# Attention stage of an attention and two-layer expert kernel: mantissa part of the weight conversion in a PSUM bank of its own

## Chip, cores and metric

One core of one Trainium2 chip. The metric is device microseconds of one launch. The kernel before took 845.74 us (median of 3 runs, 844.73 to 848.07).

## What is computed

Three stages in float32, on weights that arrive as float64:

```python
q_d, k_d, v_d = (x.reshape(B, H, Sd, 4, D).mean(axis=3) for x in (q, k, v))
out_up = np.repeat(sm_attn(q_d, k_d, v_d), 4, axis=2)
scores = np.where(abs(i - j) < 4, scale * (q @ k.T), -1e9)
x = out_up + softmax(scores) @ v
x = np.maximum(np.maximum(x @ w1, x @ w2), x @ w3) @ w_out
out = ((x @ w_a) * (x @ w_b)) @ w_out2
```

q, k and v are 4 x 8 x 576 x 64; the two later stages see 2304 tokens of width 512, with inner widths of 768 and 1536.

## The kernel before

**Stages.** Attention runs over 16 items (a batch and a pair of heads). For each item `a_load_qk` and `a_load_v` (L212 to L267) issue the loads on SP's queue, `a_qk` (L284) brings q and k into transposed form (items 0 to 7 by PE through PSUM, items 8 to 15 by DVE's transposes L291 and L292), `a_scores` (L330) makes the pooled and the windowed scores with their softmax, `a_tr` (L410) sums v over groups of four on POOL (L414, L415) and transposes the weights, and `a_av` (L445) multiplies by v and adds. Its POOL work is L396 (`ed`) and L403 (`el`, softmax by its sum), L414 and L415 (`vr`, `vd`), and L497 (`xl`, the low part of the result). One tile each of `k`, `q`, `vr` and `vw` serves items 8 to 15, so a load waits for the last reader of the item before.

**Dense work in attention.** From the fifth item on, products of the first layer (`dense`, tiles `ps_m`, L695) are put between the attention's matmuls. They need converted weights. Behind attention (from about 200 us) the order of work is written out by hand.

**Weight conversion.** `convert_steps` (L522) turns 512 columns of float64 into float32: L539 takes the exponent bits (`ce`) of the loaded tile `raw`, L542 the upper mantissa (`cm`), L546 (ACT) shifts the exponent, L547 adds the lower mantissa, L549 puts in the sign, L556 multiplies both. L561 and L562 then split the result into two parts. Eight pieces are converted in attention, one or two for each item named in `CONV_AT`. `raw` has two buffers, `ce` and `cm` one each.

**PSUM in attention.** `bk` hands out 8 banks: three under tag "t" (transposes of the weights, products with v) and five under tag "m" (transposes of q and k, scores, dense products). In the last stage `convert_steps` already keeps its mantissa in a bank, `ps_c`.

**Who sets the order.** In attention a scheduler orders the instructions of every engine by its own estimate of times and by which buffer is free; a change of buffers or of the order in `convert_steps` therefore moves other instructions too.

Of the kernel before, what the change touches and what calls it, by code (L numbers as in the profile page):

```python
# [15 lines left out]
ALU = mybir.AluOpType  # L16
# [48 lines left out]
def attn_moe_kernel(  # L65
# [14 lines left out]
    nc = tc.nc  # L80
# [47 lines left out]
    psp_ = {0: ps_ctx.enter_context(tc.tile_pool(name="psm", bufs=1, space=PSUM))}  # L128

    def bk(st, name):  # L130
        if 1 in psp_:
            return psp_[1].tile([P, 512], F32, tag="m", name=name, bufs=4)
        t, n = ("t", 3) if st in "tv" else ("m", 5)
        return psp_[0].tile([P, 512], F32, tag=t, name=name, bufs=n)


# [22 lines left out]
    for half in range(2):  # L159
        m = cap[half * 64 : half * 64 + 64]  # L160
        for sgn in (1, -1):
            nc.gpsimd.affine_select(
                out=m,
# [23 lines left out]
    st = [dict() for _ in items]  # L187
# [96 lines left out]
    def a_qk(i):  # L284
# [5 lines left out]
        if i >= TV:  # L290
# [6 lines left out]
            pool_qk(i, qp, n)  # L297
            return
        tail = bk("q", "ps_t2")
        pss = []  # L300
        for nm in ("k", "q"):
            ps = bk("q", "ps_t")
            for r in range(RF):
                nc.tensor.transpose(ps[:, r * P : (r + 1) * P], s[nm][:, r], ident)
            pss.append(ps)
# [24 lines left out]
    def a_scores(i):  # L330
        s = st[i]
        psd = bk("s", "ps_sd")
        pd = psd[: 2 * DQ, : NDQ * SD].rearrange("m (t k) -> m t k", t=NDQ)
        for t in range(NDQ):
# [187 lines left out]
    def convert_steps(key, w=None):  # L522

        r = raw.pop(key)
        lo, hi = r[:, :, 0], r[:, :, 1]
        top = r.rearrange("p n w -> p (n w)").bitcast(U16).rearrange("p (n w) -> p n w", w=4)[:, :, 3]
        late_n[0] += "p" in late
        pl = late["p"] if late_n[0] % 2 else rawp
        e = pl.tile([P, NP_], U16, tag="ce", name="ce", bufs=CB)
        fin = w  # L530
        if w is None or "c" not in psp_:
            m = pl.tile([P, NP_], F32, tag="cm", name="cm", bufs=CB)
            if w is None:
                fin = m
        if "c" in psp_:
            m = psp_["c"].tile([P, NP_], F32, tag="cs", name="ps_c", bufs=1)
        m = m.bitcast(U32)
        s16, f = e.bitcast(I16), m.bitcast(F32)
        nc.vector.tensor_scalar(  # L539
            out=e, in0=top, scalar1=0x7FF0, scalar2=None, op0=ALU.bitwise_and  # L540
        )
        nc.vector.tensor_scalar(  # L542
            out=m, in0=hi, scalar1=0x000FFFFF, scalar2=0x00100000, op0=ALU.bitwise_and, op1=ALU.bitwise_or
        )
        yield
        nc.scalar.activation(out=s16, in_=e, func=AF.Relu, bias=ebias, scale=8.0)  # L546
        nc.vector.scalar_tensor_tensor(out=f, in0=lo, scalar=2.0**-32, in1=m, op0=ALU.mult, op1=ALU.add)  # L547
        yield
        nc.vector.scalar_tensor_tensor(  # L549
            out=e, in0=top, scalar=0x8000, in1=e, op0=ALU.bitwise_and, op1=ALU.bitwise_or  # L550
        )
        yield
        i0, i1 = f, e.bitcast(BF16)
        if w is not None and len(w.shape) == 3:
            i0, i1 = (x.rearrange("p (a b) -> p a b", a=w.shape[1]) for x in (i0, i1))
        nc.vector.scalar_tensor_tensor(out=fin, in0=i0, scalar=2.0**-20, in1=i1, op0=ALU.mult, op1=ALU.mult)  # L556
        yield fin
# [6 lines left out]
    def convert_piece(key, h, l, q=None):  # L564
        for f in convert_steps(key):
            pass
        if ("q", q) in mark:
            with tc.issue_after(mark["q", q].ins):
                split(h, l, f)
        else:  # L570
            split(h, l, f)
# [70 lines left out]
    def conv1():  # L642

        key, _, h, l = inflight.pop(0)
        for f in convert_steps(key):
            if f is None:
                yield
        w_prefetch()
        yield
        nc.scalar.copy(h, f)  # L650
        yield
        nc.gpsimd.tensor_tensor(out=l, in0=f, in1=h.bitcast(F32), op=ALU.subtract)
        ready.add(key)
        yield
# [369 lines left out]
    def conv2_in(c, j):  # L1024


        def tt(eng, o, a, b, op):
            eng.tensor_tensor(out=F[:, o], in0=F[:, a], in1=F[:, b], op=op)  # L1028

        F = late["p"].tile([P, 8, KH], F32, tag="F", name="F", bufs=1)  # L1030
        for n, dst in enumerate((F[:, 0:2], F[:, 5:8:2])):
            take((2, c, j, n))
            for f in convert_steps((2, c, j, n), dst):
                yield
            ahead()
        tt(nc.vector, 3, 7, 5, ALU.add)
        tt(nc.gpsimd, 4, 0, 7, ALU.subtract)
        yield
        tt(nc.vector, 2, 3, 0, ALU.subtract)
        yield  # L1040
        tt(nc.gpsimd, 6, 1, 2, ALU.subtract)
        yield
        yield
        yield
        for g in range(2):
            if (c, j) < (1, 1):
                yield ("w", c + c + j)
            elif j == 1:
                yield ("a", 2 * c - 1, g)
            yield from split2(c, j, g, F[:, 3 * g : 3 * g + 3].rearrange("p a b -> p (a b)"))  # L1050
        yield from split2(c, j, 2, F[:, 6])
# [344 lines left out]
    for i in range(NI):  # L1396
# [4 lines left out]
        for x in LOOPS.get(i, LOOP).split():  # L1401
            f, d = x[0], int(x[1:])
# [267 lines left out]
```

## Time and profile before

| | |
|---|---|
| median of 3 runs | 845.74 us |
| profiled execution, its own time | 847.74 us |
| its span | 845.9 us |
| PE, busy share of the span | 97% |
| DVE | 78% |
| POOL | 52% |
| ACT | 42% |
| mean granted TensorE clock | 0.98 |

The span runs from the first to the last instruction of the profiled execution; 1.84 us of its time lie around it. PE is TensorE's matmuls, PEld its weight loads, DVE is VectorE, ACT is ScalarE, POOL is GpSimd, SP is the engine that issues most loads. Busy shares are means over stages with different limits, so a change to one stage is read from that stage.

### The profile page before, as it was taken

The page shows a single profiled execution, that of the slowest core. Times are in us where ns is not written, and L with a number is a line of the kernel's source. Part 1 is how long each engine was busy: PE and PEld are TensorE (multiplying, and loading weights), DVE is VectorE, ACT ScalarE, POOL GpSimd, SP SyncE. Part 2 cuts the span into 40 slices and gives each one's busy share as a digit, 9 for nine tenths or more (in the row PEclk, how much of TensorE's full clock was granted, in tenths as well). Part 3 has the DMA queues.
Part 4 walks back from the last instruction along what each step waited for, and adds up shares of the span by engine and source line. Part 5 has one row for each costly group of instructions (what it writes and reads, how often), then busy time and mean ns, then how long its engine had stood idle before and what let it go on. Part 6 is the DMA issues. An engine that isn't in the chain of part 4 may idle for free.

```text
span 845.9 us, 15426 instructions
## 1 busy us (share of the span) xinstructions
PE 818.5 (97%) x5785; PEld 767.7 (91%) x5785; DVE 656.6 (78%) x1220; ACT 355.2 (42%) x812; POOL 444.0 (52%) x417
## 2 busy tenths in 40 slices
PE   4888989999999999999999999999999999999998
PEld 3666778999999999999999999999999999999997
DVE  4899986854989688689689689798888845577775
ACT  3685654544343223324246544444433432333331
POOL 3875775445456335546557645545554543355541
PEclk8798989999999999999999999999999999999999
DMA  8997855410321111320144554454553458766612
GB/s 175 187 191 140 153 112 102 80 26 18 124 75 50 51 50 50 138 75 26 64 156 174 193 186 166 184 183 171 182 168 106 150 200 330 266 224 224 225 50 76
DMA packets 125557, 116.35 MB, mean 138 GB/s; under 512 B 81834, under 2 KB 108202, under 8 KB 125482
## 3 DMA queue, kind: packets, MB, share of 16 engines
q1 hardware_dynamic: 121162, 98.06, 39.4%
q10 hardware_dynamic: 4320, 17.30, 5.8%
q8 instruction: 45, 0.74, 0.4%
q14 instruction: 30, 0.25, 0.1%
HBM read 80.74 MB, written 34.60 MB: 136 GB/s over the span
## 4 chain that ended last, share of the span: by engine, by line
PE 85%; DMA 5%; POOL 4%; DVE 2%; SPq 2%; issue 1%; ACT 1%; POOLq 0%; DVEq 0%; ACTq 0%
PE ps_m L695 39%; PE ps_u L1086 30%; PE ps_q L860 5%; PE ps_m L1236 4%; DMA vr<-in_v_dram 4%; PE ps_av L473 1%; PE ps_ud L451 1%; POOL vr L414 1%; PE ps_tl L436 1%; POOL el L403 1%; PE ps_sd L335 1%; PE ps_s L353 1%; PE ps_m L860 1%; DMA raw<-in_moe_w_dram 1%; PE ps_td L425 1%
## 5 line engine op out<-in xcount | busy, mean ns | idle before, releaser
L695 PE MATMUL ps_m<-xh,w 128*128 128x384 f32 x864 | 175.0, 341 | 0.3 <-ACT xh L496 0.3
L695 PEld LDWEIGHTS ps_m<-xh,w 128*128 128x128 f32 x864 | 152.8, 190 | 2.1 <-ACT xh L496 0.6
L1086 PE MATMUL ps_u<-xh,w 128*128 128x384 f32 x720 | 136.8, 336 | 0.1
L1086 PEld LDWEIGHTS ps_u<-xh,w 128*128 128x128 f32 x720 | 125.3, 188 | 1.9 <-DVE acc L751 0.4
L1086 PE MATMUL ps_u<-xl,w 128*128 128x384 f32 x648 | 122.4, 335 | 0.4 <-ACT sn L1098 0.4
L1086 PEld LDWEIGHTS ps_u<-xl,w 128*128 128x128 f32 x648 | 112.9, 188 | 2.2 <-ACT sn L1098 0.7
L1098 ACT COPY sn<-ps_u 128x384 f32<-128x384 f32 x108 | 51.1, 479 | 123.7 <-PE ps_u L1086 120.2
L1276 POOL TENSOR_TENSOR gl<-g,gh 128x384 fp32r<-128x384 f32 x52 | 55.4, 1066 | 82.3 <-ACT gh L1275 75.2
L695 PE MATMUL ps_m<-xl,w 128*128 128x384 f32 x432 | 95.2, 339 | 1.7 <-POOL xl L497 1.7
L695 PE MATMUL ps_m<-wo,gh 128*128 128x512 f32 (+1 forms) x316 | 92.4, 390 | 0.0
L695 PEld LDWEIGHTS ps_m<-xl,w 128*128 128x128 f32 x432 | 76.9, 189 | 2.1 <-POOL xl L497 2.0
L695 PEld LDWEIGHTS ps_m<-wo,gh 128*128 128x128 f32 x316 | 58.4, 188 | 9.6
L724 DVE TENSOR_TENSOR t<-ps_m,t 128x384 f32<-128x384 f32 x48 | 26.5, 551 | 45.6 <-PE ps_m L695 40.3
L546 ACT ACTIVATE ce<-ce,ebias 128x512 int16<-128x512 uint16 x60 | 43.4, 724 | 43.0 <-DVE ce L539 42.9
L1017 POOL TENSOR_TENSOR w<-F,w 128x768 fp32r<-128x768 f32 (+1 forms) x36 | 56.1, 1573 | 9.2 <-ACT w L1015 8.7
L1345 DVE TENSOR_TENSOR acc<-ps_m,acc 128x512 f32<-128x512 f32 (+1 forms) x67 | 44.9, 676 | 18.1 <-PE ps_m L695 17.9
L549 DVE SCALAR_TENSOR_TENSOR ce<-raw,ce 128x512 uint16<-128x512 uint16 x60 | 49.8, 830 | 4.0 <-ACT ce L546 3.9
L1110 DVE TENSOR_TENSOR ca<-ps_u,sn 128x384 f32<-128x384 f32 x54 | 30.0, 555 | 29.4 <-PE ps_u L1086 18.1
L1028 POOL TENSOR_TENSOR F<-F 128x256 f32<-128x256 f32 x24 | 20.1, 839 | 59.3 <-DVE F L556 49.5
L695 PE MATMUL ps_m<-wo,gl 128*128 128x512 f32 (+1 forms) x158 | 48.9, 391 | 0.0
L1228 DVE TENSOR_TENSOR acc<-ps_m,acc 128x512 f32<-128x512 f32 (+1 forms) x62 | 33.3, 552 | 15.5 <-PE ps_m L1236 13.2
L539 DVE TENSOR_SCALAR ce<-raw 128x512 uint16<-128x512 uint16 x60 | 40.6, 677 | 2.2 <-DMA raw<-in_moe_w_dram 2.2
(209 smaller groups left out, 1687.4 us busy)
## 6 DMA issues: line engine op xcount, KB each, us to landing
dw<-w SPq DMA_DIRECT2D x24, 768.0 KB
raw<-in_moe_w_dram SPq DMA_DIRECT2D x18, 512.0 KB
raw<-in_moe_w_out_dram SPq DMA_DIRECT2D x18, 512.0 KB
w<-dw SPq DMA_DIRECT2D x12, 768.0 KB
w<-dw ACTq DMA_DIRECT2D x12, 768.0 KB
dw<-wo SPq DMA_DIRECT2D x12, 512.0 KB
vw<-in_v_dram SPq DMA_DIRECT2D x62, 80.0 KB
vr<-in_v_dram SPq DMA_DIRECT2D x16, 288.0 KB
```

The costliest lines, as they stand in the source:

```text
L539: nc.vector.tensor_scalar(out=e, in0=top, scalar1=0x7FF0, scalar2=None, op0=ALU.bitwise_and)
L546: nc.scalar.activation(out=s16, in_=e, func=AF.Relu, bias=ebias, scale=8.0)
L549: nc.vector.scalar_tensor_tensor(out=e, in0=top, scalar=0x8000, in1=e, op0=ALU.bitwise_and, op1=ALU.bitwise_or)
L695: nc.tensor.matmul(ps, lhs[a], rhs[b], start=(i == 0), stop=(i == n - 1))
L860: nc.tensor.matmul(ps, sw[c0, n][a][:, m * P : (m + 1) * P], hq[n][b], start=start and k == 0, stop=k == 2, skip_group_check=not start,)
L1017: nc.gpsimd.tensor_tensor(out=l, in0=w, in1=h.bitcast(F32), op=ALU.subtract)
L1086: nc.tensor.matmul(ps, w[:, a, slot, kk], y[:, b * HK + kk], start=start and i == 0, stop=i == 3 * HK - 1, skip_group_check=not start,)
L1098: nc.scalar.copy(t, ps)
L1228: nc.vector.tensor_tensor(out=a, in0=x, in1=a, op=ALU.add)
L1236: nc.tensor.matmul(y, lhs[a], tw[c, n][b], start=start and k == 0 and t == ts.start, stop=k == 2, skip_group_check=True,)
L1276: nc.gpsimd.tensor_tensor(out=l, in0=g, in1=h.bitcast(F32), op=ALU.subtract)
L1345: nc.vector.tensor_tensor(out=a, in0=ps, in1=a, op=ALU.add)
```

## The change

In attention the mantissa lies in a PSUM bank (tag "c", one buffer), the ring "m" has four banks in place of five, and the two mantissa instructions are written behind the exponent's and the sign's. Only the last multiply then writes the SBUF tile `cm`. Other stages convert as before.

```diff
-        t, n = ("t", 3) if st in "tv" else ("m", 5)
+        t, n = ("c", 1) if st == "c" else ("t", 3) if st in "tv" else ("m", 4)
...
+        attn = 1 not in psp_
+
+        def mantissa():
+            nc.vector.tensor_scalar(
+                out=m, in0=hi, scalar1=0x000FFFFF, scalar2=0x00100000, op0=ALU.bitwise_and, op1=ALU.bitwise_or
+            )
+
+        def low():
+            nc.vector.scalar_tensor_tensor(out=f, in0=lo, scalar=2.0**-32, in1=m, op0=ALU.mult, op1=ALU.add)
+
         if "c" in psp_:
             m = psp_["c"].tile([P, NP_], F32, tag="cs", name="ps_c", bufs=1)
+        elif attn:
+            m = bk("c", "ps_c")
...
-        nc.vector.tensor_scalar(
-            out=m, in0=hi, scalar1=0x000FFFFF, scalar2=0x00100000, op0=ALU.bitwise_and, op1=ALU.bitwise_or
-        )
+        if not attn:
+            mantissa()
         yield
         nc.scalar.activation(out=s16, in_=e, func=AF.Relu, bias=ebias, scale=8.0)
-        nc.vector.scalar_tensor_tensor(out=f, in0=lo, scalar=2.0**-32, in1=m, op0=ALU.mult, op1=ALU.add)
+        if not attn:
+            low()
         yield
         nc.vector.scalar_tensor_tensor(
             out=e, in0=top, scalar=0x8000, in1=e, op0=ALU.bitwise_and, op1=ALU.bitwise_or
         )
         yield
+        if attn:
+            mantissa()
+            low()
```

What the scheduler makes of it stands at three places.

DVE, from the additions behind item 3 to the transposes of item 8 (`ce`, `cm`, `ps_c` and `raw` are the conversion's tiles, `kt` and `k` the transpose's); in the kernel before:

```order
L483 TENSOR_TENSOR x_902<-ps_av,up 128x286
L539 TENSOR_SCALAR ce<-raw 128x512
L542 TENSOR_SCALAR cm<-raw 128x512
L273 TENSOR_REDUCE kd<-kt 128x144
L369 TENSOR_REDUCE md<-ps_sd 96x3
L547 SCALAR_TENSOR_TENSOR cm<-raw,cm 128x512
L549 SCALAR_TENSOR_TENSOR ce<-raw,ce 128x512
L386 TENSOR_REDUCE ml<-ps_s 128x5 x2
L291 STREAM_TRANSPOSE kt<-k 128x576
```

and now, from the same addition on:

```order
L551 TENSOR_SCALAR ce<-raw 128x512
L538 TENSOR_SCALAR ps_c<-raw 128x512
L400 TENSOR_REDUCE eps_118<-el 128x5
L315 TENSOR_REDUCE qp<-ps_t 128x128
L543 SCALAR_TENSOR_TENSOR ps_c<-raw,ps_c 128x512
L401 TENSOR_REDUCE sl<-eps_118 128x5
L561 SCALAR_TENSOR_TENSOR ce<-raw,ce 128x512
L315 TENSOR_REDUCE qp<-ps_t_1181 128x16
L273 TENSOR_REDUCE kd<-kt 128x144
L369 TENSOR_REDUCE md<-ps_sd 96x3
L402 RECIPROCAL sl<-sl 128x5
L571 SCALAR_TENSOR_TENSOR cm<-ps_c,ce 128x512
```

The fifth piece is converted as a whole before item 8's transpose, and a sixth (not shown) also stands ahead of it, where before one piece was still open.

SP, the loads around item 6's k and q (`raw` is a piece of weights); before:

```order
L518 DMA raw<-in_moe_w_dram 128x4x256
L231 DMA k<-in_k_dram 128x4x64
L243 DMA vr<-in_v_dram 72x4x256
L231 DMA k<-in_k_dram 128x4x64
L234 DMA k<-in_k_dram 64x2x64
L267 DMA vw<-in_v_dram 64x5x64 x4
L231 DMA q<-in_q_dram 128x4x64 x2
```

and now:

```order
L518 DMA raw<-in_moe_w_dram 128x4x256
L243 DMA vr<-in_v_dram 72x4x256
L267 DMA vw<-in_v_dram 64x5x64 x4
L518 DMA raw<-in_moe_w_dram 128x4x256
L231 DMA k<-in_k_dram 128x4x64 x2
L234 DMA k<-in_k_dram 64x2x64
L267 DMA vw<-in_v_dram 64x5x64 x4
L231 DMA q<-in_q_dram 128x4x64 x2
```

The sixth piece of weights (the second `raw` row) is now asked for right behind the fifth and one item's v, ahead of items 6 and 7's k and q; before it stood behind both of these. It waits for the fourth piece to be converted, since `raw` has two buffers.

PE, the scores of item 8 (`ps_s` and `ps_sd` are scores, `ps_m` dense products, all from the ring "m"); before:

```order
L335 MATMUL ps_sd<-kd,qd_92 96x144 x3
L695 MATMUL ps_m<-xh,w_141 128x384 x4
L695 MATMUL ps_m<-xl,w_140 128x384 x4
L340 LDWEIGHTS identb
L340 MATMUL ps_s<-cap,identb 128x320
L353 MATMUL ps_s<-kt,qt 58x61 x2
L353 MATMUL ps_s<-kt,qt 58x64 x3
L425 MATMUL ps_td<-ident,ed 72x96 x3
L340 LDWEIGHTS identb
L340 MATMUL ps_s<-cap,identb 128x320
L353 MATMUL ps_s<-kt,qt 58x64 x6
```

and now:

```order
L335 MATMUL ps_sd<-kd,qd_92 96x144 x3
L340 LDWEIGHTS identb
L340 MATMUL ps_s<-cap,identb 128x320
L353 MATMUL ps_s<-kt,qt 58x61 x2
L353 MATMUL ps_s<-kt,qt 58x64 x8
L340 LDWEIGHTS identb
L340 MATMUL ps_s<-cap,identb 128x320
L353 MATMUL ps_s<-kt,qt 58x64 x8
L353 MATMUL ps_s<-kt,qt 54x57 x2
```

The dense products that stood between the pooled and the windowed scores are gone from there, and one bank of scores is filled to its end before the other is begun, where before the second was opened while the first was still being written.

## Rows read from the trace of the kernel before

**Rows 1.** Stretches of the span: us, then busy us of PE, PEld, DVE, ACT, POOL; granted clock; DMA share, GB/s.

```profile
20.00:60.00 40.00, 34.24 (x463) 26.23 (x463) 37.38 (x99) 29.52 (x95) 31.02 (x31) 0.80 0.95 194
60.00:118.00 58.00, 50.60 (x640) 40.92 (x641) 55.44 (x120) 35.52 (x108) 40.78 (x45) 0.91 0.73 140
118.00:200.00 82.00, 82.00 (x960) 74.42 (x961) 51.59 (x135) 40.86 (x115) 41.02 (x50) 0.98 0.35 70
200.00:430.00 230.00, 229.01 (x1337) 227.24 (x1327) 185.93 (x308) 77.77 (x152) 118.08 (x97) 1.00 0.22 72
```

**Rows 2.** Costliest DVE groups, 0 to 120 us: busy us, mean ns of one, idle before.

```profile
L547 DVE SCALAR_TENSOR_TENSOR cm<-raw,cm 128x512 f32<-128x512 uint32 x8 | 9.8, 1231 | 0.0
L556 DVE SCALAR_TENSOR_TENSOR cm<-cm,ce 128x512 f32<-128x512 f32 x8 | 9.4, 1180 | 0.0
L539 DVE TENSOR_SCALAR ce<-raw 128x512 uint16<-128x512 uint16 x8 | 7.7, 964 | 2.2 <-DMA raw<-in_moe_w_dram 2.2
L549 DVE SCALAR_TENSOR_TENSOR ce<-raw,ce 128x512 uint16<-128x512 uint16 x8 | 6.5, 818 | 0.0
L542 DVE TENSOR_SCALAR cm<-raw 128x512 uint32<-128x512 uint32 x8 | 4.7, 586 | 0.0
```

**Rows 3.** The same groups, 430 to 700 us, where the mantissa lies in PSUM.

```profile
L547 DVE SCALAR_TENSOR_TENSOR ps_c<-raw,ps_c 128x512 f32<-128x512 uint32 x30 | 20.8, 692 | 0.7
L542 DVE TENSOR_SCALAR ps_c<-raw 128x512 uint32<-128x512 uint32 x30 | 20.5, 684 | 0.0
L556 DVE SCALAR_TENSOR_TENSOR cm<-ps_c,ce 128x512 f32<-128x512 f32 x10 | 6.8, 684 | 0.1
```

**Rows 4.** One long L547 in the timeline of DVE, then POOL beside it: start, us, what.

```profile
67.06 3.51 DVE L547 SCALAR_TENSOR_TENSOR cm<-raw,cm 128x512 f32<-128x512 uint32 x1
...
67.06 0.73 POOL L415 TENSOR_TENSOR vd<-vr 72x256 f32<-72x256 f32 x1
67.75 0.90 POOL L396 TENSOR_TENSOR ed<-ed,sd 96x432 f32<-96x432 f32 x1
68.61 1.40 POOL L403 TENSOR_TENSOR el<-el,sl 128x320 f32<-128x320 f32 x2
69.97 2.44 POOL L497 TENSOR_TENSOR xl<-x,xh 128x384 fp32r<-128x384 f32 x2
```

**Rows 5.** DVE's groups, 60 to 118 us.

```profile
L547 DVE SCALAR_TENSOR_TENSOR cm<-raw,cm 128x512 f32<-128x512 uint32 x4 | 6.8, 1694 | 0.0
L556 DVE SCALAR_TENSOR_TENSOR cm<-cm,ce 128x512 f32<-128x512 f32 x4 | 5.1, 1270 | 0.0
```

**Rows 6.** Chain of waits that ended last, 60 to 121 us: start, us, what.

```profile
68.00 2.48 issue
70.49 1.48 DVE ce L549
...
81.67 3.42 DMA vr<-in_v_dram
...
93.70 4.56 DMA vr<-in_v_dram
...
106.08 4.46 DMA vr<-in_v_dram
110.67 1.26 POOL vr L414
111.94 1.87 POOL el L403 x2
113.85 0.99 PE ps_tl L436 x5
```

**Rows 7.** Who waited for whom, 60 to 118 us: us in total, times, longest.

```profile
POOL vr L414 <- DMA vr<-in_v_dram: 14.6, 4, 6.0
PE ps_tl L436 <- POOL el L403: 3.5, 2, 3.1
PE ps_s L340 <- DVE el L387: 1.4, 2, 1.0
```

**Rows 8.** POOL's groups, 60 to 118 us, then 120 to 200 us.

```profile
L403 POOL TENSOR_TENSOR el<-el,sl 128x320 f32<-128x320 f32 x12 | 9.4, 797 | 0.0
L497 POOL TENSOR_TENSOR xl<-x,xh 128x384 fp32r<-128x384 f32 x6 | 7.1, 1182 | 0.0
...
L403 POOL TENSOR_TENSOR el<-el,sl 128x320 f32<-128x320 f32 x12 | 8.4, 719 | 0.6 <-DVE sl L402 0.6
L497 POOL TENSOR_TENSOR xl<-x,xh 128x384 fp32r<-128x384 f32 x7 | 7.3, 1050 | 0.3 <-ACT xh L496 0.2
```

## Prediction

> **What bounds the kernel now.** First the span in stretches [rows 1]. From 118 us on PE is busy without a gap (82.00 of 82 us, then 229.01 of 230), at a granted clock of 0.98 to 1.00: what attention gains or loses by then moves the end by as much. Between 60 and 118 us it is not: PE is idle for 58 - 50.60 = 7.4 us, its clock is 0.91, and DVE is busy for 55.44 of 58 us. Between 20 and 60 us the loads are the tightest: the DMA engines are busy for 0.95 of the stretch, DVE for 37.38 of 40 us. So the change, which touches DVE in attention alone, is judged in the 58 us, with a doubt about the 40 before.
>
> Second, DVE's groups in this stage [rows 2]. The five conversion instructions of a piece take 964, 586, 1231, 818 and 1180 ns in the mean. Three of them stand again in the last stage with their mantissa in PSUM, at 684, 692 and 684 ns, with hardly a spread [rows 3]. Where the long ones come from is seen in the timeline: L547 of the fifth piece begins at 67.06 us and takes 3.51 us, as long as POOL's `vd`, `ed` and `el` instructions run one behind the other (67.06 to 70.01), and ends while `xl` runs [rows 4]. L547 reads two SBUF tiles, as POOL's do; with `ps_c` it reads one.
>
> Third, the chain that ended last in the 58 us [rows 6]. It passes under this very L547 (the 2.48 us called issue from 68.00, then L549), but after 80 us it runs through the load of `vr`, three times 3.42 to 4.56 us, and through POOL's work. DVE is full, yet it isn't DVE alone that the end waits for.
>
> **The change, part by part.** Eight pieces are converted in attention, four of them between 60 and 118 us.
>
> *Mantissa in PSUM, all eight.* L542: from 4.7 us in sum to 8 x 0.684 = 5.5, so +0.8. L547: from 9.8 to 8 x 0.692 = 5.5, so -4.3. L556: from 9.4 to 8 x 0.684 = 5.5, so -3.9 [rows 2, 3]. Together 7.4 us of DVE's time. L539 and L549 write and read SBUF as before and keep their 7.7 and 6.5 us; ACT's part is the same.
>
> *The part that lies in the 58 us.* L547: 6.8 - 4 x 0.692 = 4.0. L556: 5.1 - 4 x 0.684 = 2.4 [rows 3, 5]. L542's sum there isn't in a row of its own; at its mean of 586 ns [rows 2] four take 2.3, now 2.7, so +0.4. That is 6.0 us less for DVE; the other 1.4 us lie before 60 us, where loads at 0.95 hide them: I credit nothing for these, and if the loads were not the limit there it would be up to -1.4.
>
> *What of the 6.0 us reaches the end.* On the chain I can point to one instruction: the fifth piece's L547, 3.51 - 0.69 = 2.8 us [rows 4, 6]. The other 3.2 us lie after 80 us, beside the loop of `vr`'s load and POOL. They are worth nothing as long as that loop is the limit, and all of it if DVE sets when k's and q's buffers come free. POOL gets something too: in the 58 us its `el` takes 797 ns and its `xl` 1182, against 719 and 1050 later, where no weights are converted [rows 8]. That is 12 x 0.078 + 6 x 0.132 = 1.7 us, of which L539 and L549 keep their share; I take half, 0.9 us. So 2.8 + 0.9 = 3.7 us, between 0 (all of it hidden) and 7.4 us (PE has no more idle time there).
>
> *A bank less in the ring.* Now five banks serve scores, transposes and dense products, and PE waited for DVE to empty a bank of scores 1.4 us in two waits, the longest 1.0 [rows 7]. The trace has no ring of four. From below the cost is nothing (the order now fills one bank of scores after the other, so the scheduler has gone round it); from above one wait of 1.0 us at each of the eight items that still stand before or in the 58 us, 8 us. I take one such wait near the lower end, 0.7 us (the mean of the two), because only two of them occurred with five banks and PE has other work between scores.
>
> *The new order.* Exponent before mantissa costs nothing in itself: L546 on ACT runs beside DVE's other work. But the scheduler brings pieces forward. SP asks for the sixth piece ahead of items 6 and 7's k and q, and their v behind these. The load waits for the fourth piece's conversion, and a wait on SP holds up all that stands behind it. A `vr` load of 288 KB lies on the chain with some 4.5 us [rows 6], so a piece of 512 KB that comes early can hold back what is behind it by as much, if the DMA engines are full. The same load is gone further back, and the fourth piece is converted earlier too, so I put it at nothing, with an upper bound of 4.5 us. On DVE two pieces now stand ahead of item 8's transpose instead of most of one. With L539 and L549 at their means [rows 2] and the others as in the last stage [rows 3], a piece takes 0.96 + 0.82 + 0.68 + 0.69 + 0.68 = 3.8 us, two take 7.7; before, two instructions of the one piece took 3.51 + 1.48 us [rows 4, 6]. So that transpose comes about when it did, or a little later, and the gain shows one item on.
>
> *Sum.* -3.7 + 0.7 = -3.0 us. The profiled execution, 847.74 us (span 845.9 and 1.84 around it), would become 844.7; it lies 2.0 us above the median of the runs, 845.74. On the median the forecast is **842.7 us**.
>
> **Rivals.**
>
> *Hidden.* After 80 us the loop of `vr` sets the pace: its buffer is single, POOL waited 14.6 us for four of these loads [rows 7]. POOL's order keeps that loop, and moves more of its work between a `vr` sum and the release. For it: the chain. Against it: PE waited for `el` behind it for only 3.1 us at a time. Then the change is worth 0 to 1 us: 845.4.
>
> *All of it counts.* DVE's full relief of 6.0 us and POOL's 1.7 us reach PE, up to its idle time: -7.4 us, 838.3. For it: DVE is busy for 55.44 of 58 us. The Trainium skill, "SBUF — State Buffer", section "Who interferes with whom", has VectorE and GpSimd exclude each other for a whole instruction, whichever began first, so that both gain when one side leaves the shared port; by that rule POOL's rows would fall to their later values. Against it: the DMA loop above, and L539 and L549, which stay as long as they are.
>
> *Slower: the ring of four.* While an item's scores hold three banks, dense products have one in place of two, and PE waits for DVE to empty it before the next product. The price is 1.0 us for each of eight items, 8 us, less the 3.0 us: +5.0 us, 850.7. It decides where PE's order has two dense products in a row behind scores with nothing from ring "t" between them. For it: PE had waits of this kind with five banks already [rows 7]. Against it: after 118 us PE has no idle time and its order hardly changes. The Trainium skill, "Perfetto Trace Analysis", section "Matmul Optimizations", asks for all eight PSUM banks to be at the matmuls' disposal; the change takes one away from them, and by that rule it loses.
>
> *Not as said.* That L547 and L556 stay long in spite of `ps_c` is nearly excluded: thirty of each in the last stage have means of 692 and 684 ns [rows 3].
>
> **How the numbers follow.** The forecast has 0.50, hidden 0.16, all of it 0.14, the ring or another cost of the new order 0.20. About 0.5%, 4.2 us, is what a measurement of this kernel tells from no change: faster means below 841.5, slower above 850.0. The forecast's bounds reach past 841.5 on one side, which gives 0.22 of its 0.50, the rest is no change; hidden is no change; all of it is faster; the ring is slower. So faster 0.36, same 0.44, slower 0.20. The range takes in all of it (838.3, less the 1.4 us before 60 us and 2 us for PE's clock of 0.91 in that stretch: about 835) and the ring's 850.7: 835 to 851.
>
> **What would show it.** L547 and L556 at 0.68 to 0.70 us each with hardly a spread, L542 at 0.68, L539 and L549 still with long ones among them. The chain no longer passes under a conversion at 68 us; PE's gapless stretch begins some 3 us before 118. If instead PE's waits for DVE's `el` or for emptied `ps_m` banks grow by several us, the ring is the cause; if DVE has idle time after 80 us and `vr` waits have grown, the loop of `vr` is. I'm wrong if the time is above 850 with short conversions and no new waits for banks.

## The result, and the profile after

The changed kernel takes 851.86 us (median of six runs, 849.82 to 854.55); the kernel before took 846.56 us in the six runs beside it. The ratio is 1.0061, with a 95% interval of 1.0041 to 1.0081: slower by 5.3 us, where 3.0 us less were forecast. The profiled execution has 851.4 us (span 849.6), 3.7 us more than that of before.

The conversion became short, as forecast. DVE's groups of the changed kernel, 0 to 120 us (busy us, mean ns, idle before), answer to [rows 2]:

```profile
L551 DVE TENSOR_SCALAR ce<-raw 128x512 uint16<-128x512 uint16 x8 | 10.6, 1328 | 3.3 <-DMA raw<-in_moe_w_out_dram 1.7 <-DMA raw<-in_moe_w_dram 1.6
...
L561 DVE SCALAR_TENSOR_TENSOR ce<-raw,ce 128x512 uint16<-128x512 uint16 x8 | 7.1, 889 | 0.0
...
L543 DVE SCALAR_TENSOR_TENSOR ps_c<-raw,ps_c 128x512 f32<-128x512 uint32 x8 | 5.5, 684 | 0.0
L538 DVE TENSOR_SCALAR ps_c<-raw 128x512 uint32<-128x512 uint32 x8 | 5.5, 681 | 0.0
L571 DVE SCALAR_TENSOR_TENSOR cm<-ps_c,ce 128x512 f32<-128x512 f32 x8 | 5.4, 672 | 0.1
```

L538, L543 and L571 (before: L542, L547, L556) now take what they take in the last stage [rows 3]. But L551 (before L539) went from 7.7 to 10.6 us and L561 (before L549) from 6.5 to 7.1, so the five sums fell from 38.1 to 34.1 us: 4.0 us of relief in these two profiles, not 7.4.

The stretches answer to [rows 1] (us, then busy us of PE, PEld, DVE, ACT, POOL; granted clock; DMA share, GB/s):

```profile
20.00:60.00 40.00, 31.33 (x425) 24.34 (x425) 34.41 (x92) 28.38 (x90) 28.78 (x33) 0.83 0.94 193
60.00:118.00 58.00, 50.63 (x686) 41.14 (x685) 54.91 (x127) 37.29 (x113) 35.39 (x42) 0.94 0.70 137
118.00:200.00 82.00, 80.48 (x919) 72.06 (x919) 51.10 (x132) 40.08 (x112) 42.00 (x51) 1.00 0.38 70
```

DVE lost only 0.5 us of busy time in the 58 us. The surprise is the third row: in a stretch that PE filled before, it now issues 919 products in place of 960. Who waited for whom in 60 to 118 us, against [rows 7]:

```profile
POOL vr L414 <- DMA vr<-in_v_dram: 12.6, 5, 4.4
...
PE ps_sd L335 <- ACT ed L371: 2.1, 1, 2.1
...
PE ps_tl L436 <- POOL el L403: 2.1, 1, 2.1
...
PE ps_m L710 <- ACT acc L764: 1.8, 3, 0.6
```

Two lines are waits for a bank of the ring: for `ed` to empty a bank of pooled scores, 2.1 us, and for emptied dense banks, 1.8 us. The wait for `el` has shrunk from 3.5 to 2.1 us.

Where attention ends is seen in the group of the value products of each kernel (durations, then first and last start). Before, then after:

```profile
L473 PE MATMUL ps_av<-pt,vw x640: 215/218/355, 31.2 to 200.3; 64*64 64x58 f32 x151, 64*64 64x54 f32 x9
```

```profile
L473 PE MATMUL ps_av<-pt,vw x640: 212/218/355, 32.7 to 203.7; 64*64 64x58 f32 x152, 64*64 64x54 f32 x8
```

The last value product begins 3.4 us later; behind it both kernels need the same, 845.9 - 200.3 = 645.6 and 849.6 - 203.7 = 645.9 us. So the loss lies ahead of 204 us. It lies behind 140 us, too. Eleven of the sixteen items have their value products behind them at 140.6 us before and at 140.3 us after, with 160 and 162 dense products done. First the dense products `ps_m`, then the score products `ps_s` (bias products included), up to that point and from there to the end of attention (us, busy us of PE, count; clock, DMA share, GB/s), before:

```profile
0.00:140.60 140.60, 36.55 (x160) 0.88 0.78 155
140.60:200.50 59.90, 41.34 (x213) 1.00 0.26 54
...
0.00:140.60 140.60, 24.84 (x504) 0.88 0.78 155
140.60:200.50 59.90, 4.95 (x168) 1.00 0.26 54
```

and after:

```profile
0.00:140.30 140.30, 33.99 (x162) 0.91 0.77 154
140.30:203.90 63.60, 40.76 (x211) 1.00 0.27 54
...
0.00:140.30 140.30, 25.24 (x504) 0.91 0.77 154
140.30:203.90 63.60, 7.64 (x168) 1.00 0.27 54
```

Nearly the same work takes 63.6 in place of 59.9 us, at the full clock in both, and 2.69 of the 3.7 us are one row: 168 score products take 7.64 instead of 4.95 us. The first 140 us come out even at different clocks. Before, PE waited 3.1 us for `el`, up to 113.9 us, and was then granted the lower level (1.2 GHz) for part of the next microseconds; after, it had the upper level (2.4 GHz) throughout. The same 10 us, before and then after:

```profile
110.00:120.00 10.00, 6.87 (x64) 5.15 (x61) 8.85 (x19) 4.93 (x16) 9.32 (x10) 0.71 0.57 122
110.00:120.00 10.00, 9.14 (x131) 7.46 (x130) 9.24 (x28) 5.65 (x19) 7.42 (x10) 1.00 0.60 113
```

How the score products became slower, the timeline of PE shows at item 12 (start, us, what). Before:

```profile
145.97 0.43 PE L340 MATMUL ps_s<-cap,identb 128*128 128x320 bf16 x2
146.33 0.79 PE L353 MATMUL ps_s<-kt,qt 64*58 64x61 f32 x40
```

After:

```profile
146.15 0.30 PE L340 MATMUL ps_s<-cap,identb 128*128 128x320 bf16 x1
146.38 0.76 PE L353 MATMUL ps_s<-kt,qt 64*58 64x61 f32 x18
147.08 0.31 PE L340 MATMUL ps_s<-cap,identb 128*128 128x320 bf16 x1
147.32 0.77 PE L353 MATMUL ps_s<-kt,qt 64*58 64x64 f32 x22
```

Before, both banks get their bias and 40 score products (20 in the program, two passes each) follow in 0.79 us. After, one bank is written but for two passes, then the other, and 18 products take as long as 40 did. The code suggests why: a score product uses 64 rows and at most 58 columns of the array, and `order_s` deals them out over four quarters of it, head by rows, half by columns. A bank alone holds products for two of the quarters, so neighbours in the order have two quarters to share instead of four. The Trainium skill, "TensorEngine Tiling (Array Packing)", section "Key Properties", states that different tiles can run their matmuls in parallel; these rows agree, 0.79 us for 40 products in four quarters against 1.53 us for the same 40 in two quarters at a time. That the order makes them slower is shown below (e5, e6). Which limit does it is argued only: a bank and its two quarters always go together here, so no run tells apart a lack of quarters and a limit of products in a row that write the same bank.

### The profile page after: what moved, and what is told of

Read it like the earlier page. It is cut to its first block, busy times and chain, and to the rows that moved or that the text cites. A ratio compares the mean times of both kernels' runs of the same rounds, so it can differ in the third digit from the quotient of the medians.

```text
span 849.6 us, 15460 instructions
## 1 busy us (share of the span) xinstructions
PE 817.9 (96%) x5785; PEld 766.7 (90%) x5785; DVE 654.0 (77%) x1220; ACT 357.1 (42%) x812; POOL 437.1 (51%) x417
## 4 chain that ended last, share of the span: by engine, by line
PE 84%; DVE 8%; SPq 2%; DMA 2%; issue 2%; POOL 1%; ACT 1%; DVEq 0%; POOLq 0%; ACTq 0%
PE ps_m L710 39%; PE ps_u L1101 30%; PE ps_q L875 5%; PE ps_m L1251 4%; DVE ce L551 1%; PE ps_s L353 1%; PE ps_av L473 1%; SPq L223 1%; PE ps_ud L451 1%; PE ps_sd L335 1%; PE ps_m L875 1%; DMA raw<-in_moe_w_out_dram 1%; DVE ce L561 1%; DMA raw<-in_moe_w_dram 1%; PE ps_tl L436 1%
## 5 line engine op out<-in xcount | busy, mean ns | idle before, releaser
L710 PE MATMUL ps_m<-xh,w 128*128 128x384 f32 x864 | 172.7, 338 | 0.7 <-DVE el L387 0.4
L561 DVE SCALAR_TENSOR_TENSOR ce<-raw,ce 128x512 uint16<-128x512 uint16 x60 | 50.5, 841 | 4.0 <-ACT ce L557 3.9
L551 DVE TENSOR_SCALAR ce<-raw 128x512 uint16<-128x512 uint16 x60 | 43.6, 727 | 3.3 <-DMA raw<-in_moe_w_out_dram 1.7
```

The source lines that it names most:

```text
L551: nc.vector.tensor_scalar(out=e, in0=top, scalar1=0x7FF0, scalar2=None, op0=ALU.bitwise_and)
L561: nc.vector.scalar_tensor_tensor(out=e, in0=top, scalar=0x8000, in1=e, op0=ALU.bitwise_and, op1=ALU.bitwise_or)
L710: nc.tensor.matmul(ps, lhs[a], rhs[b], start=(i == 0), stop=(i == n - 1))
```

## Experiments

In ten of them (e1 to e7, e12 to e14) the order is pinned: a table holds the order that the scheduler made for another kernel, and each instruction of attention gets an edge to its predecessor on its engine (issue order only, no wait). It stands ahead of the stage that is ordered by hand, and moves line numbers by up to 8:

```diff
+ORDER = {
...
+}
...
+    for eng, seq in ORDER.items():
+        mine = [x for x in traced if str(x.engine) == "EngineType." + eng]
+        for x, y in zip(seq, seq[1:]):
+            tc.add_manual_dep(
...
     ctx.enter_context(tc.manual_schedule())
```

Pinning alone, with nothing else changed, wasn't run. The nearest is e14, the kernel before pinned with whole score products, at 1.0004 (0.9983 to 1.0024): a price of pinning could hide there only behind an equal gain. One thing needed no run: with the mantissa written first in the program again, the scheduler issues the same order on all five engines as for the changed kernel, and in the kernel before with the exponent first, the order of before. So "exponent part first" has no part in what follows (e2, e5, e7, e8, e12 and e13 write the mantissa first again); what differs is the ring and the bank.

**Ring alone, in the order of before (e1).**

```diff
-        t, n = ("t", 3) if st in "tv" else ("m", 5)
+        t, n = ("t", 3) if st in "tv" else ("m", 4)
```

> The kernel before, its order of instructions on every engine pinned as it is, with the ring of transposes, scores and dense banks cut from five to four; the mantissa stays in SBUF. Theory order (the loss of 5.3 us comes from the new order that the scheduler makes, not from waits for banks): within 1.0 us of before, about 846 to 848. Theory ring (the lost bank itself makes TensorE wait, in any order): 850 to 853, and PE's waits for ring banks between 20 and 120 us grow from some 2 to 3 us to 6 us or more. Theory conversion (the mantissa in PSUM is what costs): 846.5, as before.

Measured: 851.79 us against 846.85, ratio 1.0055 (1.0036 to 1.0073). Theory order failed; theory ring is right for this order. PE's waits of e1 in 60 to 118 us:

```profile
PE ps_m L703 <- ACT ed L379: 4.2, 3, 2.6
PE ps_s L348 <- DVE t L732: 1.8, 1, 1.8
PE ps_m L703 <- DVE t L732: 1.3, 1, 1.3
PE ps_s L348 <- DVE el L395: 0.8, 1, 0.8
```

All four are waits for a bank, 8.1 us together; before, there were 1.4 us for `ps_s` [rows 7] and 0.5 us for a dense bank.

**The whole change in the order of before (e2):** e1 with `ps_c` from a bank of its own, as in the change.

> The whole change (mantissa in a PSUM bank, ring of four) with the order of before pinned on every engine. Theory order: the forecast's own sum comes true, 843 to 845 (3 us below before), since short conversions are left and the new order is gone. Theory ring: 848 to 852, 3 us less than ring four alone in this order. Theory conversion: as much above e1 as the change is above before, 5 us, 851 or more.

Measured: 847.81 us against 846.85, ratio 1.0000 (0.9979 to 1.0022). The time lies between the ranges of theory order and theory ring, in neither of them. The PSUM bank gives back 0.55%, 4.7 us, what the ring of four takes. The same work in the scheduler's new order is the changed kernel, at 1.0061: the order alone makes the change a loss.

**The new order alone (e3):** order of the changed kernel pinned, `("m", 5)`, and the mantissa in SBUF:

```diff
+        if 1 not in psp_:
+            m = ap_.tile([P, NP_], F32, tag="mm", name="mm", bufs=1)
         m = m.bitcast(U32)
```

> The order of the changed kernel pinned on every engine, with five banks in the ring and the mantissa in an SBUF tile of its own: nothing of the change is left but the order. Theory order: 851 to 855, as slow as the changed kernel or 3 us slower, the long conversions being back. Theory ring: 846 to 849, about the kernel before. Theory conversion: 846.5.

Measured: 853.12 us, ratio 1.0068 (1.0046 to 1.0090): theory order.

**The new order with the ring of four (e4):** e3 with `("m", 4)`.

> The changed kernel's order and its ring of four, but the mantissa in an SBUF tile of its own. Theory order: equal to e3 within 1 us. Theory ring: 3 to 6 us above e3, and 0 to 3 us above the changed kernel. Theory conversion: 5 us below the changed kernel, 846 to 847. What the PSUM bank is worth in this order is the difference to the changed kernel; the forecast had it at 3 us.

Measured: 854.52 us, ratio 1.0089 (1.0066 to 1.0111). In this order the ring costs 0.21%, 1.8 us, less than the 3 to 6 us of theory ring and more than the 1 us of theory order. The PSUM bank gives 0.28%, 2.4 us, against the changed kernel; each of these two ratios is known to 0.2%, so that difference isn't quite clear of noise. Side by side, as ratios to before:

| | ring 5, SBUF | ring 4, SBUF | ring 4, PSUM |
|---|---|---|---|
| order of before | 1 | 1.0055 (e1) | 1.0000 (e2) |
| order of the change | 1.0068 (e3) | 1.0089 (e4) | 1.0061 (the change) |

**The split of the score products, undone (e5).** The changed kernel's order pinned, but on PE the 22 instructions of each of items 12 to 15 in the order of the program. PE's row of the table is made so (`G[n]` are an item's 22 instructions):

```python
for n in (12, 13, 14, 15):
    pos = [i for i, x in enumerate(seq) if x in G[n]]
    for q, x in zip(pos, sorted(G[n])):
        seq[q] = x
```

> The changed kernel with its own order pinned on every engine, but for the score products of the last four items (12 to 15) on TensorE: there the two bias products and the twenty score products stand as the program writes them, both banks interleaved, instead of one bank's half after the other's. Theory split (TensorE, never idle there, works on two quadrants of its array instead of four: 1.84 to 1.94 us an item instead of 1.15 to 1.49, read from the trace): 2.7 us below the changed kernel, about 849. Theory waits (the loss sits in waits of the first eight items alone, and the second half has slack): as the changed kernel, 852.

Measured: 849.41 us against 848.14, ratio 1.0010 (0.9990 to 1.0031), against 1.0061 for the change: 4.3 us less by the ratios, each known to about 1.8 us. Without the split of these four items the new order isn't told from the old one any more, with the same ring and bank: 1.0010 here, 1.0000 in e2. The score products of the four items in e5:

```profile
146.80:149.20 2.40, 1.15 (x42) 1.00 0.31 71
160.30:163.00 2.70, 1.15 (x42) 1.00 0.04 8
174.30:177.00 2.70, 1.15 (x42) 1.00 0.03 6
188.70:191.40 2.70, 1.16 (x42) 1.00 0.00 0
```

**The split, put into the kernel before (e6).** The order of before pinned, ring of five, mantissa in SBUF, with the split order for the same four items.

> The kernel before (ring of five, mantissa in SBUF), its own order pinned, with the score products of items 12 to 15 in the changed kernel's order, one bank's half after the other's. Theory split: 2.7 us above before, about 849.5. Theory waits: as before, 846.8.

Measured: 850.52 us against 848.14, ratio 1.0026 (1.0007 to 1.0045), 2.2 us more. The rows of e6:

```profile
144.60:148.00 3.40, 1.93 (x42) 1.00 0.03 6
158.90:162.00 3.10, 1.93 (x42) 1.00 0.26 50
173.20:177.00 3.80, 1.94 (x42) 1.00 0.02 4
187.70:192.00 4.30, 1.83 (x42) 1.00 0.00 0
```

So the split is shown from both sides: 2.2 and 4.3 us in the time, each known to some 2 us, and 2.69 us in PE's rows.

**The bank from the other ring (e7):** e2 with `("t", 2)` and `("m", 5)`.

> The mantissa in a PSUM bank of its own, taken from the other ring (transposes of the weights and values: two banks instead of three), the ring of transposes and scores back at five, the order of before pinned. By e1 and e2 the ring of four costs 4.9 us in that order and the PSUM bank gives 4.0 back. If ring t has a bank to spare: 843. If it has not: its waits (PE for POOL's el and for the copies of the transposed weights) add 3 us or more, 846 to 850.

Measured: 857.61 us against 848.14, ratio 1.0106 (1.0080 to 1.0132), above both ranges. Ring "t" has no bank to spare: in 18 to 200 us PE's transposes of the pooled weights wait for DVE to empty a bank of value products.

```profile
PE ps_td L433 <- DVE x L491: 12.5, 9, 3.2
```

**The mantissa as a guest in the ring of five (e8).**

```diff
-        t, n = ("c", 1) if st == "c" else ("t", 3) if st in "tv" else ("m", 4)
+        t, n = ("t", 3) if st in "tv" else ("m", 5)
```

> The mantissa in a bank drawn from the ring of transposes and scores, which stays at five banks; no bank of its own; the scheduler orders anew, and keeps the score products of items 10 to 15 whole. Theory split and ring: 843 to 847, since neither the split nor a permanent loss of a bank is there, and conversions are short. Theory that any new order costs: 850 or more.

Measured: 853.72 us against 848.14, ratio 1.0062 (1.0038 to 1.0086). Score products are whole behind 118 us, and yet it is slower: my theory missed. This new order loses earlier; in 18 to 200 us PE waits for ACT's `pt` 3.5 us in one piece, which it didn't before (for POOL's `el` it waits 4.6 us, before 5.3). Which decision of the scheduler brings the loss is open.

**The ring alone, scheduler free (e9):** e1 without the pin.

> The kernel before with the ring of transposes and scores cut from five banks to four and nothing else; the scheduler orders anew. Its order has the second bank's bias product behind the first bank's score products in items 9 to 15. Theory split (a fourth bank that is late in the scheduler's own plan makes it write the score products bank by bank): the split items, alone in TensorE's full stretch behind 118 us, cost some 0.7 us each, 4 us, so 850 to 855, and the score products take 1.7 us or more an item there. Theory PSUM order (the new order comes from the mantissa's bank): 846 to 849, score products whole in 1.15 us.

Measured: 855.95 us against 847.44, ratio 1.0101 (1.0073 to 1.0129), just above the 850 to 855 us of theory split. The ring of four alone makes the scheduler split; item 12 in e9, where before had 1.15 us:

```profile
149.00:152.00 3.00, 1.82 (x42) 1.00 0.00 0
```

**The change with the score products chained (e10).**

```diff
+        mm = [x for x in nc.cur_bb.bb.instructions[n0:] if str(x.engine) == "EngineType.PE"]
+        for x, y in zip(mm, mm[1:]):
+            tc.add_manual_dep(
...
         ed = s["ed"] = pool(i, 3).tile([2 * DQ, NDQ, SD], F32, tag="ed", bufs=1 if pool(i, 3) is ex else 2, name="ed")
```

> The changed kernel, with one addition: each item's two bias products and twenty score products are chained in the written order on TensorE, so that the scheduler can't take them apart; it orders all else anew. Theory split: as e5 or better, 846 to 849, score products in 1.15 us an item from item 11 on. Theory that any new order with four banks costs in the first 140 us: 850 or more with whole score products.

Measured: 850.67 us against 847.44, ratio 1.0045 (1.0027 to 1.0063). The scheduler makes yet another order, in which whole scores wait for a bank that DVE's `el` must empty (18 to 210 us):

```profile
PE ps_s L341 <- DVE el L396: 5.5, 4, 3.6
```

and it puts other products between the two bias products of items 11, 12, 14 and 15. So the time is that of the second theory, with another new order; what part of the loss lies in the first 140 us isn't shown.

**The same chain in the kernel before (e11).**

> The kernel before (five banks, mantissa in SBUF) with the same chain of score products in every item. Behind 118 us its score products are whole already, but for 0.34 us of item 13; what is new is items 1, 4, 7, 8 and 9. Theory split alone: 0 to 2 us below before. Theory that any new order costs: 2 to 5 us above.

Measured: 853.36 us, ratio 1.0073 (1.0050 to 1.0096). Two to five were foreseen for "any new order costs"; it is 6.2 us by the ratio, though ring, mantissa and conversion are those of before. In 18 to 210 us PE waits 7.9 us for POOL's `el` and 4.4 us for `xl`; before, in 18 to 200 us, these were 5.3 and 1.7 us.

**e2 with all score products whole (e12):** the loop of e5 over all items, on the order of before.

> e2 (mantissa in its PSUM bank, ring of four, order of before pinned) with the score products of all items whole on TensorE: items 1, 4, 7, 8, 9 and 13 change. 0.34 us of item 13 is sure; in the first 118 us TensorE waits, so the other five (0.8 us each at the full clock) give back at most 4 us if none of them waits for its second bank: 843.5 to 847.5. If they wait for the second of four banks: 848 to 852.

Measured: 845.52 us against 847.44, ratio 0.9992 (0.9971 to 1.0012): not to be told from before. PE still waits for a bank, in 18 to 210 us:

```profile
PE ps_m L713 <- ACT ed L379: 4.4, 2, 3.1
```

**Those two waits taken away (e13):** in e12's order, 3 and 9 dense products put behind the value products that followed them.

> e12 (order of before pinned, ring of four, mantissa in PSUM, score products whole) with two groups of dense products (3 and 9) moved on TensorE behind the value products that follow them. In e12 these two groups wait 4.4 us for ScalarE's exponentials to empty the pooled scores' bank, while the value products behind them have their operands 1.4 and 1.25 us earlier. Theory waits (the ring of four costs at these places): 2 to 3 us below e12, 842 to 844, the forecast's 842.7. Theory spread (DVE or POOL sets the end of the stage, PE only waits elsewhere): as e12, 845 to 846.

Measured: 848.60 us against 848.08, ratio 1.0012 (0.9984 to 1.0040), above both ranges, though not clear of e12's 0.9992. Theory waits failed: nothing gained. The wait for `ed` fell to 2.4 us, and others came. PE's largest waits of e13, 18 to 210 us:

```profile
PE ps_tl L444 <- POOL el L411: 3.1, 2, 2.1
PE ps_m L713 <- ACT ed L379: 2.4, 2, 1.8
PE ps_sd L343 <- DVE el L395: 2.1, 1, 2.1
PE ps_s L348 <- DVE t L742: 1.6, 1, 1.6
PE ps_m L713 <- DVE t L742: 1.6, 1, 1.6
```

The first is a wait for an operand; the other four are banks that DVE or ACT empties late. In this one attempt the wait for a bank moved and didn't go.

**The kernel before with whole score products, pinned (e14).**

> The kernel before, its order pinned, with the score products of all items whole: ring of five, mantissa in SBUF. Theory split: 0.3 us of item 13 for sure and up to 2 us in the first 118 us, so 844.5 to 847 where before is 847. If e12 owes its 2.3 us below e2 to noise: as before.

Measured: 847.83 us against 848.08, ratio 1.0004 (0.9983 to 1.0024). Splits in the first 118 us cost nothing that shows; PE has idle time there (7.4 of 58 us in [rows 1]). The 2.3 us of e12 below e2 aren't confirmed by this run.

No version beats both kernels: e12 is level with before, 0.7% below the changed kernel by the ratios.

## Why the prediction was wrong

*Conversion, 3.7 us.* The direction was right and the size not far off: e1 against e2 gives 4.7 us in the order of before, e4 against the change 2.4 us in the new one. The forecast's 7.4 us of relief for DVE are there where the order is kept: the five sums (0 to 125 us) are 37.9 us in e1 and 30.7 in e2. In the changed kernel they fell by 4.0 us alone, since "L539 and L549 ... keep their 7.7 and 6.5 us" doesn't hold there. The longest L551, in the timeline of DVE, then POOL beside it (answers to [rows 4]):

```profile
72.31 2.84 DVE L551 TENSOR_SCALAR ce<-raw 128x512 uint16<-128x512 uint16 x1
...
71.96 1.54 POOL L497 TENSOR_TENSOR xl<-x,xh 128x384 fp32r<-128x384 f32 x2
73.46 0.72 POOL L415 TENSOR_TENSOR vd<-vr 72x256 f32<-72x256 f32 x1
74.14 0.72 POOL L403 TENSOR_TENSOR el<-el,sl 128x320 f32<-128x320 f32 x1
```

It ends 0.3 us behind these four POOL instructions, though it reads one SBUF tile only. But that the moved mantissa makes it long isn't shown. The mean of the eight exponent instructions differs from kernel to kernel: 725 to 1462 ns in the eight profiles with the mantissa in SBUF (e9 725, before 964, e6 1462), 861 to 1726 ns in the eight with `ps_c` (e5 861, the changed kernel 1328, e13 1726). In the order of before with `ps_c` (e2) it is:

```profile
L559 DVE TENSOR_SCALAR ce<-raw 128x512 uint16<-128x512 uint16 x8 | 8.2, 1026 | 1.6 <-DMA raw<-in_moe_w_dram 1.6
```

The sign that "the chain no longer passes under a conversion at 68 us" holds for 68 us only; against [rows 6], the chain of the changed kernel passes under two others:

```profile
65.22 1.62 DVE ce L551
...
72.39 2.76 DVE ce L551
```

PE's gapless stretch didn't begin 3 us earlier either: behind 118 us PE is busy for 80.48 of 82 us.

*A bank less, 0.7 us.* Mis-sized, within its bounds of 0 and 8 us. In the order of before it costs 4.7 us (e1), in the new one 1.8 us (e3 to e4). I took the low end because "the order now fills one bank of scores after the other, so the scheduler has gone round it". That sentence holds the mistake: going round it was what cost most.

*The new order: "I put it at nothing".* This step failed. By e3 the order alone costs 0.68%, 5.8 us (3.9 to 7.6), where I gave 4.5 us as its upper bound, and I looked for it at the wrong place, in SP's loads and DVE's conversions. The difference on PE stood in the rows on the change. I read them for waits and didn't price what they do to PE's own speed. The terms as measured in the new order are 5.8 + 1.8 - 2.4 = 5.2 us; that they meet the result, 5.3, proves nothing, since by their making they are the steps from before over e3 and e4 to the changed kernel. What e5 and e6 add is that the split of items 12 to 15 is 2 to 4 us of it.

*"From 118 us on PE is busy without a gap".* I used this as a reason that nothing is lost there (the ring rival has "its order hardly changes"). It is the opposite: where PE is full, a slower way to issue the same products moves the end by all of it. Of the profiled 3.7 us, 2.69 are the split scores of items 12 to 15; the other 1.0 us behind 140 us has no single row. The first 140 us came out even, 140.3 against 140.6, though DVE was relieved and TensorE was granted 0.91 in place of 0.88. So something was lost there too; the ring's waits and the rest of the new order are what is left, and how it divides between them wasn't settled.

*The rivals.* The ring of four had the right sign and nearly the right time (850.7) at a chance of 0.20. Its mechanism, dense products that wait for a bank, is what happens if the order is kept (e1); it is not what the changed kernel does, where the scheduler, short of a bank, takes the scores apart (e9 shows that the ring alone makes it do so). Its page, the Trainium skill's "Perfetto Trace Analysis", section "Matmul Optimizations", asks for all eight banks; e1, 0.55% slower with one bank less, agrees. In e2 DVE has that bank, and what the matmuls lose is given back: 1.0000. "Hidden" and "all of it" fell: the relief does reach the end (e2). "Wrong if above 850 with short conversions and no new waits for banks" was half met: PE's waits for a bank in 60 to 118 us grew from 1.9 to 4.8 us, but the larger part of the loss is no wait at all.

## What to carry to other kernels

Where a scheduler orders the instructions, a change of a pool's size is a change of the order, and the order can have its price: five kernels that it ordered anew (the change, e8 to e11) were all slower, by 0.45 to 1.01%. In e11 the edit itself was harmless, since whole score products in the old order cost nothing (e14). All five are measured against one order, that of before, which may have been a lucky one; that any new order costs isn't shown. Compare the order instruction by instruction where the bound engine is full, and price what it does to that engine's own rate, not only its waits: here, small products in quarters of the array ran at half the rate when they were issued bank by bank. To judge the edit itself, pin the old order (e1, e2).

## What the runs showed of the hardware

- The same 40 score products take 0.79 us with both banks interleaved and 0.76 + 0.77 us bank by bank, at the full granted clock; a busy PE row hides a factor of two. Whether the quarters or the bank set it isn't shown.
- A DVE instruction with one SBUF input (L551, 128x512 uint16; 0.42 us at its shortest in the changed kernel) took 2.84 us beside four POOL instructions in a row. The Trainium skill, "SBUF — State Buffer", section "Who interferes with whom", counts `tensor_scalar` among those that can take the port shared with GpSimd; the row agrees. How often it is held differs from kernel to kernel: over the sixteen profiles its mean was 725 to 1726 ns, and the kernels with the mantissa in SBUF and in PSUM overlap widely.
- The same kernel with four banks in two orders loses 4.7 or 1.8 us to the missing bank (e1; e3 to e4): what a bank is worth seems to depend on the order too.
